# Forward and gradients of a spectral block with an MLP: gradient products laid beside the spectral passes, gelu and slope in one pass, transposes by DMA

## The chip, the cores and the metric

One core of a Trainium2 chip runs the whole program once. The metric is the device time in microseconds (us), as the median of several runs. TensorE (PE) multiplies, VectorE (DVE), ScalarE (ACT) and GpSimd (POOL) work on tiles, and SP, ACT and POOL issue transfers.

## The reference

The kernel computes the block, all in bf16 at its borders, and the gradient of every input but the MLP's own x, for an incoming `grad_out` (S = 2048 tokens, D = 1024, F = 3584):

```python
sa, ca, ga, sb, cb, gb = rows of silu(c) @ w_mod
h  = layernorm(x) * (1 + ca) + sa
x1 = x + ga * irfft2(rfft2(h) * (w_r + 1j * w_i))
h2 = layernorm(x1) * (1 + cb) + sb
out_0 = x1 + gb * (gelu_tanh(layernorm(h2) @ w1 + b1) @ w2 + b2)
# out_1 .. out_9: gradients of x, w_r, w_i, w1, b1, w2, b2, c, w_mod
```

## The kernel before

The spectral filter is done with products: tokens and columns are folded into even and odd parts, a cosine or sine matrix is multiplied from both sides, and the spectrum is handled in eight pairs of row blocks. `spectral` (L357 on) does it for the forward and for the backward: `prep_chunk` and the folds for four chunks of 512 tokens, `s_fwd` (L398, 128 products "pu"), eight times `pair` (L419, products "pcs", then the multiplication by w on DVE; in the backward also the gradients of w), `s_inv` (L484, 128 products "pv"), and for four chunks the products "po" (L511), their copies to `o4` (L513), the unfolding and `consume_chunk`. In the forward, `consume_fwd` (L556 on) forms x1, two layernorms and n3, and stores A, x1, n2 and n3 to DRAM.

The MLP stages follow one after the other, each with its own pools, so that a stage's tiles stand where an earlier one's stood. Six of them have 896 products of 128x512 each:
- z = n3 @ w1 (L623), over four token blocks of 512 and seven groups of four row tiles; n3 is transposed on PE (L103). gelu is done there; z, the sigmoid and gelu's value are stored as d_zb, d_sg and d_hh, and `transpose_sf` (L118 to L122) transposes gelu's value on PE into d_hhs.
- the w2 product (L662), with w2 in SBUF, out_0, and gBo = grad_out * gb.
- gz (L745): gBo times w2 transposed; d_zb and d_sg are loaded again, gelu's slope is computed, `gz` is stored as d_gz and, transposed on PE, as d_gzs.
- the gradients of w2 (L807) and of w1 (L831).
- the gradient of n3 (L859) with `ln_bwd_tile` (L700 to L708).

Then `spectral` runs backward, and `gmod_part` (L761 on; three calls, one of them ahead of L807) forms the gradients of w_mod (L773, an outer product on ACT) and c (L775, a reduction on DVE) from the six rows that stand in d_gmod. The code's order is each engine's order; SP and ACT share the loads, POOL has most stores; w1T and w2T come by DMA transposes on ACT's queue (L786, L687).

Of the kernel before, what the change touches and what calls it, by code (L numbers as in the profile page):

```python
# [10 lines left out]
FP32 = mybir.dt.float32  # L11
# [6 lines left out]
P = 128  # L18
S = 2048
# [16 lines left out]
def kernel(  # L36
# [51 lines left out]
    d_sg = dram.tile([F, S], BF16, name="d_sg")
    d_hhs = dram.tile([S, F], BF16, name="d_hhs")
    d_gzs = dram.tile([S, F], BF16, name="d_gzs")  # L90
    d_gmod = dram.tile([6 * D], FP32, name="d_gmod")
    d_zb_v = d_zb.rearrange("(fc p) s -> p fc s", p=P)
    d_sg_v = d_sg.rearrange("(fc p) s -> p fc s", p=P)
# [3 lines left out]
    def srows(dt, t):  # L97
        return dt[t * P:(t + 1) * P, :]

    def transpose8(src):  # L100
        pt = psum.tile([P, NDC * P], BF16, tag="tr", name="pt")
        for cc in range(NDC):
            nc.tensor.transpose(pt[:, cc * P:(cc + 1) * P], src[:, cc * P:(cc + 1) * P], ident[:])  # L103
        return pt

    def transpose_into(dstT, col0, src):
        pt = transpose8(src)
        nc.vector.tensor_copy(out=dstT[:, 0:NDC, col0:col0 + P],  # L108
                              in_=pt[:, :].rearrange("p (c k) -> p c k", k=P))

    def transpose_sf(wk, src4, d_dst, blk, g):
        stg = wk.tile([P, 4, 4 * P], BF16, tag="stg")
        for ip in range(2):
            pt = psum.tile([P, 2, 4 * P], BF16, tag="pc", name="pts")
            for ii in range(2):
                i = ip * 2 + ii
                for k in range(4):
                    nc.tensor.transpose(pt[:, ii, k * P:(k + 1) * P], src4[:, k, i * P:(i + 1) * P], ident[:])  # L118
            if ip == 0:
                nc.scalar.copy(out=stg[:, 0:2, :], in_=pt[:])  # L120
            else:
                nc.vector.tensor_copy(out=stg[:, 2:4, :], in_=pt[:])  # L122
        nc.sync.dma_start(out=d_dst[blk * BW:(blk + 1) * BW, g * BW:(g + 1) * BW].rearrange("(i p) f -> p i f", p=P),
                          in_=stg[:])

    def store_gmod(wk, accs, r):
        for h in range(2):
            row = wk.tile([1, KH], FP32, tag="gmrow")
            nc.vector.tensor_copy(out=row[:], in_=accs[h][0:1, :])  # L129
            nc.sync.dma_start(out=d_gmod[r * D + h * KH:r * D + (h + 1) * KH].rearrange("(o n) -> o n", o=1), in_=row[:])  # L130

    modx = ExitStack()
    modp = modx.enter_context(tc.tile_pool(name="modp", bufs=1))
    modrows = modp.tile([P, 6, D], BF16, name="modrows")
    modrows_b = const.tile([P, 4, D], BF16, name="modrows_b")
    modcols = const.tile([P, 6, NDC], FP32, name="modcols")
# [3 lines left out]
    with tc.tile_pool(name="modw", bufs=2) as mw:  # L140
        c_bf = mw.tile([P, NDC], BF16, name="c_bf", bufs=1)
        with nc.allow_non_contiguous_dma(reason="tiny c load"):
            nc.sync.dma_start(out=c_bf[:], in_=c.rearrange("o (j p) -> p (o j)", p=P))
        nc.vector.tensor_copy(out=c_col[:], in_=c_bf[:])
        nc.scalar.activation(out=sigc[:], in_=c_col[:], func=ACT.Sigmoid)
        nc.vector.tensor_tensor(out=u_col[:], in0=c_col[:], in1=sigc[:], op=ALU.mult)
        u_b = mw.tile([P, NDC, P], BF16, name="u_b", bufs=1)
        nc.gpsimd.memset(u_b[:], 0.0)
        for jc in range(NDC):
            nc.vector.tensor_scalar(out=u_b[:, jc, :], in0=u_b[:, jc, :], scalar1=u_col[:, jc:jc + 1],  # L150
                                    scalar2=None, op0=ALU.add)
        modraw = mw.tile([P, 6, D], BF16, name="modraw", bufs=1)
        for cb in range(12):
            wblk = mw.tile([P, NDC, KH], BF16, tag="wblk", bufs=3)
            (nc.sync, nc.gpsimd, nc.scalar)[cb % 3].dma_start(
                out=wblk[:], in_=w_mod[:, cb * KH:(cb + 1) * KH].rearrange("(j p) n -> p j n", p=P))
            pm = psum.tile([P, KH], FP32, tag="pa", name="pm")
            for jc in range(NDC):
                nc.tensor.matmul(pm[:], lhsT=u_b[:, jc, :], rhs=wblk[:, jc, :], start=(jc == 0), stop=(jc == NDC - 1))
            nc.scalar.copy(out=modraw[:, cb // 2, (cb % 2) * KH:(cb % 2 + 1) * KH], in_=pm[:])  # L160
        for r in range(6):
            if r in (1, 4):
                nc.vector.tensor_scalar(out=modrows[:, r, :], in0=modraw[:, r, :], scalar1=1.0, scalar2=None,
                                        op0=ALU.add)
            else:
                nc.scalar.copy(out=modrows[:, r, :], in_=modraw[:, r, :])
        pcol = psum.tile([P, 6 * NDC], FP32, tag="pb", name="pcol")
        for r in range(6):
            for dc in range(NDC):
                nc.tensor.matmul(pcol[:, r * NDC + dc:r * NDC + dc + 1], lhsT=modrows[0:1, r, dc * P:(dc + 1) * P],  # L170
                                 rhs=ones_bf[0:1, 0:1], start=True, stop=True)
        nc.vector.tensor_copy(out=modcols[:].rearrange("p r c -> p (r c)"), in_=pcol[:])
    sa_row = modrows[:, 0, :]
    opca_row = modrows[:, 1, :]
    ga_row = modrows[:, 2, :]
    sb_row = modrows[:, 3, :]
    opcb_row = modrows[:, 4, :]
    gb_row = modrows[:, 5, :]
    nc.scalar.copy(out=modrows_b[:, 0, :], in_=modrows[:, 1, :])
    nc.scalar.copy(out=modrows_b[:, 1, :], in_=modrows[:, 4, :])  # L180
    nc.scalar.copy(out=modrows_b[:, 2, :], in_=modrows[:, 5, :])
    nc.scalar.copy(out=modrows_b[:, 3, :], in_=modrows[:, 2, :])
    opca_row_b = modrows_b[:, 0, :]
    opcb_row_b = modrows_b[:, 1, :]
    gb_row_b = modrows_b[:, 2, :]

    d_P = dram.tile([8, P, 4 * PW], BF16, name="d_P")
    d_SF = dram.tile([P, 4, 4, 512], BF16, name="d_SF")
    d_SI = dram.tile([P, 4, 4, 512], BF16, name="d_SI")
    d_E = dram.tile([P, 2, 8, 256], BF16, name="d_E")  # L190
    d_G = dram.tile([P, 2, 8, 256], BF16, name="d_G")
    CE, CO, SE, SO = 0, 1, 2, 3

    with tc.tile_pool(name="dft", bufs=1) as dftp, tc.tile_pool(name="gen", bufs=2) as gen:
        SFg = dftp.tile([P, 4, 4, 512], BF16, name="SFg")
        SIg = dftp.tile([P, 4, 4, 512], BF16, name="SIg")
# [12 lines left out]

        kev = to_f(iota_f([[128, 4], [64, 2], [-1, 64]], 64, 0, 512, "kev"), 512, "kev")  # L210
# [798 lines left out]
```

## Time and profile before

| | us |
|---|---|
| median of three runs (2504.49 to 2512.33) | 2506.34 |
| the profiled execution | 2504.36 |
| its span | 2502.6 |
| PE busy | 1629.9 |
| DVE busy | 1222.0 |
| ACT busy | 622.3 |
| POOL busy | 249.1 |

The span runs from the first to the last instruction of the profiled execution; an engine's busy time leaves out waits. No engine is busy over the whole span, so it has to be read by stages.

### The profile page before, as it was taken

The page shows a single profiled execution, that of the slowest core. Times are in us where ns is not written, and L with a number is a line of the kernel's source. Part 1 is how long each engine was busy: PE and PEld are TensorE (multiplying, and loading weights), DVE is VectorE, ACT ScalarE, POOL GpSimd, SP SyncE. Part 2 cuts the span into 40 slices and gives each one's busy share as a digit, 9 for nine tenths or more (in the row PEclk, how much of TensorE's full clock was granted, in tenths as well). Part 3 has the DMA queues.
Part 4 walks back from the last instruction along what each step waited for, and adds up shares of the span by engine and source line. Part 5 has one row for each costly group of instructions (what it writes and reads, how often), then busy time and mean ns, then how long its engine had stood idle before and what let it go on. Part 6 is the DMA issues. An engine that isn't in the chain of part 4 may idle for free. (4 is left out here: it accounts for less than half of the span.)

```text
span 2502.6 us, 21021 instructions
## 1 busy us (share of the span) xinstructions
PE 1629.9 (65%) x7779; PEld 757.4 (30%) x7928; DVE 1222.0 (49%) x1759; ACT 622.3 (25%) x736; POOL 249.1 (10%) x375
## 2 busy tenths in 40 slices
PE   3108610189983899879995989788889953754200
PEld 1004310044441344334442434333334420322100
DVE  4465776355551111289990000000136557597784
ACT  2304310055551000065540000000012220312332
POOL 1000010011110111111000000111100000030000
PEclk7559855599996999989997989899989985867655
DMA  6643254576669543487779231333165335343355
GB/s 207 171 159 114 89 215 154 193 235 222 224 219 263 155 139 106 138 299 259 254 229 220 83 101 68 130 99 99 43 186 171 105 78 151 115 113 115 121 179 173
DMA packets 295659, 400.06 MB, mean 160 GB/s; under 512 B 98038, under 2 KB 221944, under 8 KB 294276
## 3 DMA queue, kind: packets, MB, share of 16 engines
q1 hardware_dynamic: 153044, 188.32, 24.7%
q0 software_dynamic: 47792, 144.84, 16.5%
q10 hardware_dynamic: 94720, 65.55, 9.9%
q8 instruction: 62, 1.02, 0.2%
q14 instruction: 41, 0.34, 0.0%
HBM read 212.90 MB, written 167.83 MB: 152 GB/s over the span
## 5 line engine op out<-in xcount | busy, mean ns | idle before, releaser
L807 PE MATMUL gw2acc<-gbo_all,hhs 128*128 128x512 bf16 x878 | 210.3, 401 | 42.8 <-ACT ot L813 25.2
L662 PE MATMUL pbo<-w_sb,hhb 128*128 128x512 bf16 x878 | 206.3, 387 | 33.5 <-DMA x1t<-d_x 26.0
L831 PE MATMUL gw1acc<-gzs,n_all 128*128 128x512 bf16 x878 | 202.2, 388 | 29.7 <-DMA gzs<-d_gzs 13.2
L859 PE MATMUL pg<-w1T,gzb 128*128 128x512 bf16 x880 | 200.7, 383 | 19.9 <-DMA gzb<-d_gz 18.9
L623 PE MATMUL pz<-n3T,w_sb 128*128 128x512 bf16 x868 | 204.8, 390 | 5.3 <-DVE n3T L108 3.1
L745 PE MATMUL ph<-gBoT,w2T 128*128 128x512 bf16 x868 | 201.6, 380 | 2.8 <-DVE gBoT L108 1.2
L398 PE MATMUL pu<-smat,fbuf 128*128 128x512 bf16 x251 | 64.9, 416 | 122.5 <-DMA smat<-d_SF 76.6
L807 PEld LDWEIGHTS <-hhs 128*128 128x128 bf16 x896 | 91.2, 102 | 161.6 <-issue 66.3
L814 DVE CAST ot<-gw2acc 128x512 bf16<-128x512 f32 x28 | 18.7, 689 | 237.4 <-PE gw2acc L807 193.5
L831 PEld LDWEIGHTS <-n_all 128*128 128x128 bf16 x896 | 89.3, 100 | 142.7 <-issue 43.7
L662 PEld LDWEIGHTS <-hhb 128*128 128x128 bf16 x896 | 87.6, 100 | 143.4 <-issue 38.1
L859 PEld LDWEIGHTS <-gzb 128*128 128x128 bf16 x896 | 88.2, 99 | 127.4 <-issue 23.0
L838 DVE CAST ot<-gw1acc 128x512 bf16<-128x512 f32 x28 | 19.4, 692 | 217.6 <-PE gw1acc L831 141.5
L623 PEld LDWEIGHTS <-w_sb 128*128 128x128 bf16 x896 | 88.5, 100 | 108.2 <-issue 10.8
L103 PE MATMUL pt<-ident,n3t 128*128 128x128 bf16 x128 | 12.9, 277 | 164.7 <-DMA n3t<-d_n 164.6
L745 PEld LDWEIGHTS <-w2T 128*128 128x128 bf16 x896 | 85.9, 98 | 94.9 <-issue 2.0
L625 ACT ACTIVATE zb<-pz,b_col 128x512 bf16<-128x512 f32 x112 | 75.4, 684 | 111.1 <-PE pz L623 107.1
L484 PE MATMUL pv<-smi,R 128*128 128x512 bf16 x248 | 67.3, 421 | 32.3 <-DVE R L453 18.4
L679 DVE TENSOR_TENSOR gbo<-go,modrows_b 128x1024 bf16<-128x1024 bf16 x16 | 11.1, 693 | 150.9 <-DMA go<-in_grad_out_dram 150.9
L667 ACT CAST bo<-pbo 128x512 bf16<-128x512 f32 x32 | 18.7, 586 | 251.8 <-PE pbo L665 203.4
L813 ACT CAST ot<-gw2acc 128x512 bf16<-128x512 f32 x28 | 15.7, 587 | 237.7 <-PE gw2acc L807 148.1
L398 PEld LDWEIGHTS <-fbuf 128*128 128x128 bf16 x256 | 25.8, 104 | 161.6 <-issue 83.7
(602 smaller groups left out, 2555.7 us busy)
## 6 DMA issues: line engine op xcount, KB each, us to landing
d_zb<-zb POOLq DMA_DIRECT2D x28, 512.0 KB, 5.2
d_sg<-sg POOLq DMA_DIRECT2D x28, 512.0 KB, 3.4
d_hhs<-stg SPq DMA_DIRECT2D x28, 512.0 KB
sg<-d_sg ACTq DMA_DIRECT2D x28, 512.0 KB
zb<-d_zb SPq DMA_DIRECT2D x28, 512.0 KB
d_gz<-gz POOLq DMA_DIRECT2D x28, 512.0 KB, 4.5
d_gzs<-stg SPq DMA_DIRECT2D x28, 512.0 KB
x<-in_A_x_dram SPq DMA_DIRECT2D x32, 256.0 KB
```

The costliest lines, as they stand in the source:

```text
L398: nc.tensor.matmul(pu[:], lhsT=fbuf[:, i, cl, c8 * P:(c8 + 1) * P], rhs=smat[:, cl, i, :], start=(i == 0), stop=(i == 3))
L484: nc.tensor.matmul(pv[:], lhsT=R[:, cl * 4 + m, :, :].rearrange("p x w -> p (x w)")[:, base:base + 255:2], rhs=smi[:, cl, m, :], start=(m ...
L623: nc.tensor.matmul(pz[:], lhsT=w1_sb[:, cch, fc * P:(fc + 1) * P], rhs=n3T[:, cch, :], start=(cch == 0), stop=(cch == NDC - 1))
L625: nc.scalar.activation(out=zb[:, k, :], in_=pz[:], func=ACT.Identity, bias=b1_col[:, fc:fc + 1], scale=1.0)
L662: nc.tensor.matmul(pb_[:], lhsT=hhbs[fc // HF][:, fc % HF, i * P:(i + 1) * P], rhs=w2_sb[:, fc, h * KH:(h + 1) * KH], start=(fc == 0), sto ...
L667: nc.scalar.copy(out=bo[:, h * KH:(h + 1) * KH], in_=pb_[:])
L745: nc.tensor.matmul(ph[:], lhsT=w2T[:, cch, fc * P:(fc + 1) * P], rhs=gBoT[:, cch, :], start=(cch == 0), stop=(cch == NDC - 1))
L807: nc.tensor.matmul(accs[k * 2 + h][:], lhsT=hhs[:, t, k * P:(k + 1) * P], rhs=gbo_all[:, t, h * KH:(h + 1) * KH], start=(t == 0), stop=(t ...
L814: nc.vector.tensor_copy(out=ot[:, KH:D], in_=accs[k * 2 + 1][:])
L831: nc.tensor.matmul(accs[cch][:], lhsT=n3_all[:, t, cch * P:(cch + 1) * P], rhs=gzs[:, t, :], start=(t == 0), stop=(t == NT - 1))
L838: nc.vector.tensor_copy(out=ot[:], in_=accs[cch][:])
L859: nc.tensor.matmul(pg[:], lhsT=gzb[:, fc, i * P:(i + 1) * P], rhs=w1T[:, fc, h * KH:(h + 1) * KH], start=(fc == 0), stop=(fc == NFC - 1))
```

## The change

The file is rewritten, with the same arithmetic in other places:
- All SBUF tiles come from one pool `reg` with tags set by hand, so that a tile of a later stage waits only for the tile whose tag it takes; the tile framework's scheduler orders each engine. PSUM has 2 + 2 + 4 banks under the tags s, d and f.
- gBo and its transposes come first. The product with w2 transposed (`pp`, L573) is placed beside the forward spectral pass and stored as d_ph. POOL generates the matrices' angles.
- `z_block` (L599) computes z, gelu, gelu's slope and gz in one pass; `bo_pass` (L635) runs the w2 product for one block and one half of the columns between z blocks and loads w2 again each time (28 MB in all).
- the gradient of n3 (L720) has the layernorm gradients and the backward fold in its loop. The gradient of w2 (L817) stands after the backward spectral pass in the code, and the scheduler mixes it with that pass's consume. The w_mod gradients (L859, L861) stand ahead of the gradient of w1 (L887).
- n1 and n2 are not stored but computed again; layernorm sums run on ACT (`ln_act`).
- There are no PE transposes: n3, gBo, w1, w2, d_hh and d_gz come transposed by DMA. All transfers but POOL's are on SP.

```diff
-                        nc.scalar.activation(out=zb[:, k, :], in_=pz[:], func=ACT.Identity,
...
-                    nc.scalar.activation(out=sg[:], in_=u_[:], func=ACT.Sigmoid, scale=2.0 * GK)
...
-                    transpose_sf(wk, hh, d_hhs, blk, g)
...
-                        nc.vector.tensor_tensor_reduce(out=gz[:, k, :], in0=ph[:], in1=dd[:, k, :], scale=1.0, scalar=0.0,
...
-                    transpose_sf(wk, gz, d_gzs, blk, g)
...
+    for fg in range(F // 256):
+        w2t = wt[:, fg % 2]
+        nc.sync.dma_start_transpose(out=w2t, in_=B_w2[fg * 256:(fg + 1) * 256, :])
+        for b in range(NB):
...
+            for k in range(2):
...
+                    nc.tensor.matmul(pp[:], lhsT=w2t[:, cch, k * P:(k + 1) * P], rhs=gBoT[b][:, cch, :],
...
+                nc.scalar.copy(out=ph2[:, k, :], in_=pp[:])
...
+            nc.sync.dma_start(out=ph, in_=d_ph_v[:, g * 4:(g + 1) * 4, b * BW:(b + 1) * BW])
...
+            nc.scalar.activation(out=av, in_=zb, func=ACT.Square)
+            nc.vector.tensor_scalar(out=av, in0=av, scalar1=GC, scalar2=1.0, op0=ALU.mult, op1=ALU.add)
+            tt(bv, av, zb, ALU.mult)
+            nc.scalar.activation(out=sg, in_=bv, func=ACT.Sigmoid, scale=2.0 * GK)
+            nc.scalar.activation(out=bv, in_=bv, func=ACT.Sigmoid, scale=-2.0 * GK)
+            nc.vector.tensor_scalar(out=av, in0=av, scalar1=6.0 * GK, scalar2=-4.0 * GK, op0=ALU.mult, op1=ALU.add)
+            tt(hh, sg, zb, ALU.mult)
...
+    z_block(0, 0, 7)
+    bo_pass(0, 0)
+    for b in range(1, NB):
+        z_block(b, 0, 4)
+        bo_pass(b - 1, 1)
+        z_block(b, 4, 7)
+        bo_pass(b, 0)
+    bo_pass(NB - 1, 1)
...
+        nc.sync.dma_start_transpose(out=hhs, in_=d_hh[fg * 256:(fg + 1) * 256, :])
...
+            nc.scalar.activation(out=gw, in_=grep_, func=ACT.Copy, scale=u_rt[:, jc:jc + 1])
...
+        nc.sync.dma_start_transpose(out=gzs, in_=d_gz[fg * 512:(fg + 1) * 512, :])
```

How the orders differ at three places. First PE in the forward consume. Before, the last of the products "po" on the inverse spectrum V are followed by the PE transposes of n3's rows (n3t):

```order
L511 MATMUL po<-gneg,V 128x256
L511 LDWEIGHTS V
L511 MATMUL po<-gneg,V 128x256
L103 LDWEIGHTS n3t
L103 MATMUL pt<-ident,n3t 128x128
```

Now PE has the "pp" products (weights w2 transposed, `wt`) up to the first "po" of the next chunk:

```order
L573 MATMUL pp<-gBoT_340,wt 128x512
L573 LDWEIGHTS wt
L573 MATMUL pp<-gBoT_340,wt 128x512
L464 LDWEIGHTS V_1200
L464 MATMUL po<-gm,V_1200 128x256
L464 LDWEIGHTS V_1200
```

Some 94 "pp" products stand ahead of each of the three later chunks, 68 ahead of the main "pu" run, and 344 in one piece behind the last chunk.

Second, the transposes of w1. Before, ACT's queue issued them between the end of gz and the first copies of the w2 gradient:

```order
L120 COPY stg<-pts 128x1024 x2
L771 DMA wrow<-in_w_mod_dram 128x1024
L786 DMA_TRANSPOSE w1T<-in_B_w_dram 128x1024 x4
L120 COPY stg<-pts 128x1024
L786 DMA_TRANSPOSE w1T<-in_B_w_dram 128x1024 x24
L813 CAST ot<-gw2acc_7965 128x512
```

Now they are on SP, among the last w2 loads of the w2 product (w2sA, w2sB, w2sC):

```order
L694 DMA_TRANSPOSE w1T_5735<-in_B_w_dram 128x1024 x2
L643 DMA w2sA<-in_B_w_dram 128x4x512
L694 DMA_TRANSPOSE w1T_5735<-in_B_w_dram 128x1024
L694 DMA_TRANSPOSE w1T_5740<-in_B_w_dram 128x1024
L643 DMA w2sB<-in_B_w_dram 128x4x512
L694 DMA_TRANSPOSE w1T_5740<-in_B_w_dram 128x1024 x3
```

Third, ACT at the w_mod gradients. Before, they stood at the end of its order, behind the last layernorm gradients (L707), with their own loads:

```order
L773 ACTIVATE gw<-grep__13311,u_rt 128x3072
L707 ACTIVATE tmp<-n_13242,sc 128x1024 x4
L771 DMA wrow<-in_w_mod_dram 128x3072 x2
L771 DMA wrow<-in_w_mod_dram 128x2048
L773 ACTIVATE gw<-grep__13371,u_rt 128x2048 x3
```

Now the 48 outer rows (gww) stand between the first and the second copy of the w1 gradient (gwo):

```order
L837 ACTIVATE sr<-accSA_9560 1x512
L837 ACTIVATE sr<-accSA_9561 1x512
L891 CAST gwo_9802<-gw1acc 128x512
L859 ACTIVATE gww<-gr_9576,u_rt 128x1024 x8
L859 ACTIVATE gww<-gr_9577,u_rt 128x1024 x8
```

Four more such groups of eight follow, and then the other 27 copies in one piece. On DVE, too, few of its 28 copies (L893) stand ahead of its 48 reductions (L861).

More of the change, by code (lines that the diff above doesn't have):

```diff
@@ L88 @@
[L88 to L93, printed above, removed]
-    d_hh_v = d_hh.rearrange("(fc p) s -> p fc s", p=P)
-    d_gz_v = d_gz.rearrange("(fc p) s -> p fc s", p=P)
[L97 to L135, printed above, removed]
@@ L136 @@
-    modcols = const.tile([P, 6, NDC], FP32, name="modcols")
+    rows4 = const.tile([P, 4, D], BF16, name="rows4")
+    opca_row, ga_row, opcb_row, gb_row = (rows4[:, r, :] for r in range(4))
+    stats = const.tile([P, 3, 2, NT], FP32, name="stats")
+    gb1_acc = const.tile([P, NFC, NB], FP32, name="gb1_acc")
     u_col = const.tile([P, NDC], FP32, name="u_col")
@@ L139 @@
     c_col = const.tile([P, NDC], FP32, name="c_col")
[L140 to L184, printed above, removed]
@@ new lines, in tt, with store_gmod, colsum @@
+    def tt(out, a, b, op):
+        nc.vector.tensor_tensor(out=out, in0=a, in1=b, op=op)
+    def store_gmod(accs, r):
+        for h in range(2):
+            row = small.tile([1, KH], FP32, tag="gmrow", bufs=1)
+            nc.vector.tensor_copy(out=row[:], in_=accs[h][0:1, :])
+            nc.sync.dma_start(out=d_gmod[r * D + h * KH:r * D + (h + 1) * KH].rearrange("(o n) -> o n", o=1), in_=row[:])
+    def colsum(accs, src, first, last):
+        for h in range(2):
+            nc.tensor.matmul(accs[h][:], lhsT=ones_bf[:], rhs=src[:, h * KH:(h + 1) * KH], start=first, stop=last)
@@ new lines @@
+    c_bf = small.tile([P, NDC], BF16, tag="c_bf", bufs=1)
+    b1_bf = small.tile([P, NFC], BF16, tag="b1_bf", bufs=1)
+    with nc.allow_non_contiguous_dma(reason="tiny column loads"):
+        nc.sync.dma_start(out=c_bf[:], in_=c.rearrange("o (j p) -> p (o j)", p=P))
+        nc.gpsimd.dma_start(out=b1_bf[:], in_=B_b1.rearrange("(f p) -> p f", p=P))
+    nc.vector.tensor_copy(out=b1_col[:], in_=b1_bf[:])
+    nc.vector.tensor_copy(out=c_col[:], in_=c_bf[:])
+    nc.scalar.activation(out=sigc[:], in_=c_col[:], func=ACT.Sigmoid)
@@ new lines, with mod_block @@
+    MOD_DST = {0: sar[:, 0, 0, :], 1: opca_row, 2: ga_row, 3: sb_row, 4: opcb_row, 5: gb_row}
+    wblkA = reg.tile([P, 4, NDC, KH], BF16, name="wblkA", tag="fr")
+    def mod_block(r, h, wblk):
+        cb = 2 * r + h
+        nc.sync.dma_start(out=wblk, in_=w_mod[:, cb * KH:(cb + 1) * KH].rearrange("(j p) n -> p j n", p=P))
+        pm = ps_f("pm")
+        for jc in range(NDC):
+            nc.tensor.matmul(pm[:], lhsT=u_b[:, jc, :], rhs=wblk[:, jc, :], start=(jc == 0), stop=(jc == NDC - 1))
+        dst = MOD_DST[r][:, h * KH:(h + 1) * KH]
+        nc.scalar.copy(out=dst, in_=pm[:])
+        if r in (1, 4):
+            nc.vector.tensor_scalar(out=dst, in0=dst, scalar1=1.0, scalar2=None, op0=ALU.add)
@@ new lines, in ln_act @@
+    def ln_act(x4, row, i, jk):
+        sv = small.tile([P, 4, 4], FP32, tag="lnsv")
+        for q in range(4):
+            nc.scalar.activation(out=jk[:, q, :], in_=x4[:, q, :], func=ACT.Identity, accum_out=sv[:, q, 0:1])
+        nc.vector.tensor_scalar(out=sv[:, :, 1:2], in0=sv[:, :, 0:1], scalar1=-1.0 / D, scalar2=None, op0=ALU.mult)
+        for q in range(4):
+            nc.scalar.activation(out=jk[:, q, :], in_=x4[:, q, :], func=ACT.Square, bias=sv[:, q, 1:2], accum_out=sv[:, q, 2:3])
+        ln_fin(sv[:, :, 2:3], sv[:, :, 1:2], sv[:, :, 3:4], 1.0 / D, row, i)
@@ new lines, in ln_fin, with ln_dve @@
+    def ln_fin(var, nmean, std, scale, row, i):
+        nc.scalar.activation(out=std, in_=var, func=ACT.Sqrt, bias=eps_c[:], scale=scale)
+        rs = stats[:, row, 0, 4 * i:4 * i + 4].rearrange("p (q o) -> p q o", o=1)
+        nc.vector.reciprocal(out=rs, in_=std)
+        tt(stats[:, row, 1, 4 * i:4 * i + 4].rearrange("p (q o) -> p q o", o=1), nmean, rs, ALU.mult)
+    def ln_dve(x4, row, i):
+        st = small.tile([P, 4, 2, nc.vector.BN_STATS_DIM], FP32, tag="lnst")
+        mv = small.tile([P, 4, 4], FP32, tag="lnmv")
@@ new lines, in ln_dve, with norm_act, s_fwd @@
+        ln_fin(mv[:, :, 1:2], mv[:, :, 2:3], mv[:, :, 3:4], 1.0, row, i)
+    def norm_act(out4, in4, row, i):
+        for q in range(4):
+            t = 4 * i + q
+            nc.scalar.activation(out=out4[:, q, :], in_=in4[:, q, :], func=ACT.Identity,
+                                 scale=stats[:, row, 0, t:t + 1], bias=stats[:, row, 1, t:t + 1])
+    def s_fwd(cl, fb, sm, evac):
+        Ut = reg.tile([P, 8, 512], BF16, name=f"U{cl}", tag=f"uv{cl}")
+        for c8 in range(8):
+            pu = ps_s("pu")
+            for i in range(4):
+                nc.tensor.matmul(pu[:], lhsT=fb[:, i, cl, c8 * P:(c8 + 1) * P], rhs=sm[:, i, :],
+                                 start=(i == 0), stop=(i == 3))
+            evac(Ut[:, c8, :], pu[:])
+        return Ut
@@ new lines @@
+    for fg in range(F // 256):
+        hhs = hhs2[fg % 2]
+        nc.sync.dma_start_transpose(out=hhs, in_=d_hh[fg * 256:(fg + 1) * 256, :])
+        for k in range(2):
+            fc = 2 * fg + k
+            ob = gwo[:, fc % 2]
+            for h in range(2):
+                acc = ps_f("gw2acc")
+                for t in range(NT):
+                    nc.tensor.matmul(acc[:], lhsT=hhs[:, t, k * P:(k + 1) * P], rhs=gBs[t // 4][:, t % 4, h * KH:(h + 1) * KH],
+                                     start=(t == 0), stop=(t == NT - 1))
+                nc.scalar.copy(out=ob[:, h * KH:(h + 1) * KH], in_=acc[:])
+            nc.gpsimd.dma_start(out=out_6[fc * P:(fc + 1) * P, :], in_=ob)
@@ new lines @@
+    accGA = [ps_f("accGA0"), ps_f("accGA1")]
+    for b in range(NB):
+        gxa = reg.tile([P, 4, D], BF16, name="gxa", tag=f"uv{2 * (b % 2)}")
+        ata = reg.tile([P, 4, D], BF16, name="ata", tag=f"uv{2 * (b % 2) + 1}")
+        nc.sync.dma_start(out=gxa[:], in_=chunk_rows(d_gx1, b))
+        nc.sync.dma_start(out=ata[:], in_=chunk_rows(d_A, b))
+        tt(gxa[:], gxa[:], ata[:], ALU.mult)
+        for q in range(4):
+            colsum(accGA, gxa[:, q, :], b == 0 and q == 0, b == 3 and q == 3)
@@ new lines @@
+    for fg in range(F // 512):
+        gzs = gzs2[:, fg % 2]
+        nc.sync.dma_start_transpose(out=gzs, in_=d_gz[fg * 512:(fg + 1) * 512, :])
+        for cch in range(NDC):
+            acc = ps_f("gw1acc")
+            for t in range(NT):
+                nc.tensor.matmul(acc[:], lhsT=n3ns[t // 4][:, t % 4, cch * P:(cch + 1) * P], rhs=gzs[:, t, :],
+                                 start=(t == 0), stop=(t == NT - 1))
+            ob = gwo1[:, (fg * NDC + cch) % 4]
+            if cch % 2 == 0:
+                nc.scalar.copy(out=ob, in_=acc[:])
+            else:
+                nc.vector.tensor_copy(out=ob, in_=acc[:])
+            nc.gpsimd.dma_start(out=out_4[cch * P:(cch + 1) * P, fg * 512:(fg + 1) * 512], in_=ob)
```

1306 lines of the change are left out of this document (593 added, 713 removed).

## The prediction

> **What bounds the kernel now.** I read the page's head, then a table of busy time by stage that I cut at the changes of line in TensorE's (PE's) timeline, then the groups, then single waits.
>
> ```profile
> span 2502.6 us, 21021 instructions
> PE 1629.9 (65%) x7779; PEld 757.4 (30%) x7928; DVE 1222.0 (49%) x1759; ACT 622.3 (25%) x736; POOL 249.1 (10%) x375
> ```
>
> No engine is full over the span: PE idles 873 us. In the table the columns are the stretch, its length, busy time of PE, weight loads, DVE, ACT, POOL, then PE's granted clock, DMA share and GB/s.
>
> ```profile
> 0.00:194.00 194.00, 40.75 (x161) 14.57 (x165) 101.60 (x186) 37.08 (x43) 14.91 (x23) 0.61 0.59 174
> 194.00:297.00 103.00, 90.31 (x417) 47.17 (x423) 66.00 (x94) 45.73 (x82) 4.29 (x8) 0.94 0.34 111
> 297.00:487.00 190.00, 12.81 (x73) 8.87 (x72) 127.36 (x192) 13.09 (x29) 14.61 (x17) 0.54 0.51 185
> 487.00:773.00 286.00, 244.47 (x1441) 126.44 (x1469) 148.53 (x155) 153.09 (x169) 42.17 (x56) 0.91 0.68 223
> 773.00:1046.00 273.00, 228.30 (x976) 95.68 (x995) 42.17 (x66) 19.38 (x33) 27.78 (x42) 0.92 0.50 139
> 1046.00:1317.00 271.00, 235.75 (x1444) 120.30 (x1471) 248.21 (x399) 142.30 (x91) 30.33 (x46) 0.95 0.80 263
> 1317.00:1583.00 266.00, 210.57 (x884) 91.28 (x899) 19.97 (x31) 16.73 (x29) 23.87 (x38) 0.87 0.44 118
> 1583.00:1821.00 238.00, 202.21 (x878) 89.26 (x896) 19.37 (x28) 16.41 (x28) 34.74 (x61) 0.94 0.29 96
> 1821.00:2134.00 313.00, 233.53 (x984) 99.85 (x1004) 187.46 (x287) 62.77 (x97) 13.96 (x19) 0.85 0.45 132
> 2134.00:2260.00 126.00, 90.66 (x347) 42.46 (x353) 93.14 (x125) 36.68 (x65) 31.57 (x50) 0.81 0.45 118
> 2260.00:2400.00 140.00, 39.01 (x182) 21.16 (x185) 109.59 (x134) 52.44 (x61) 5.05 (x5) 0.62 0.39 136
> 2400.00:2502.00 102.00, 1.55 (x4) 0.30 (x2) 58.64 (x66) 26.57 (x14) 5.84 (x11) 0.50 0.50 169
> ```
>
> Row by row: head; forward transforms; forward consume; z; w2 product; gz; gw2; gw1; gn3 with the backward fold; backward transforms; backward consume; grad-w_mod tail. Six product stages are PE's; head, both consumes and tail leave it 153, 177, 101 and 100 us idle.
>
> ```profile
> 486.91 1.33 PE L103 MATMUL pt<-ident,n3t 128*128 128x128 bf16 x11 [144.79 <-DMA n3t<-d_n]
> 580.65 6.42 PE L623 MATMUL pz<-n3T,w_sb 128*128 128x512 bf16 x28
> ```
>
> The first row is the largest single wait: 144.79 us. The second gives the steady product: 6.42/28 = 0.229 us, so each 896-matmul stage costs 205 us.
>
> **The change, in stages.** *Removed:* the gz stage as a stage (271 us), since its product goes under the forward spectral pass, and these PE transposes (39.9 us busy; 12.9 and 11.0 us of L103's go too):
>
> ```profile
> L118 PE MATMUL pts<-ident,gz 128*128 128x128 bf16 x448 | 39.9, 224 | 23.0 <-DVE gb_acc L747 21.9
> ```
>
> *Head, 150 us (130 to 180; was 194).* The forward matrix no longer goes out to d_SF and back:
>
> ```profile
> L398 PE MATMUL pu<-smat,fbuf 128*128 128x512 bf16 x251 | 64.9, 416 | 122.5 <-DMA smat<-d_SF 76.6 <-DVE fbuf L383 29.9 <-DVE fbuf L273 14.8
> ```
>
> Of that 76.6 us I take 44 back, because four gBo transposes and 68 pp products now stand ahead of the main pu run.
>
> *Transforms, 112 us (103 to 130; was 103).* A pair is two products of 2052 columns and six of about half that on DVE, 2 x 1.23 + 6 x 0.69 = 6.6 us:
>
> ```profile
> L445 DVE TENSOR_TENSOR qb<-Pt,ws 128x2052 bf16<-128x2052 bf16 x16 | 19.7, 1229 | 0.0
> L447 DVE TENSOR_TENSOR Q<-qa,qb 128x1026 bf16<-128x1026 bf16 x16 | 11.1, 694 | 0.0
> ```
>
> So 128 pu at 0.229 are 29, eight pairs 53, 128 pv 29. PE's pp work fits in the pairs' gaps; without that cover it would be late by what stands there, some 110 products or 25 us, which is the upper end.
>
> *Forward consume, 218 us (190 to 260; was 190).* Here a serial chain of ACT and DVE, a chunk at a time, is the pace, since o4 and x4 have one buffer each. On ACT, now the engine of the mean, square and normalising passes, these rows price it:
>
> ```profile
> L513 ACT CAST o<-po 128x512 bf16<-128x512 f32 x64 | 33.6, 619 | 69.9 <-DMA out_dram<-o 33.4 <-DMA d_A<-o 29.7 <-DMA out_dram<-gw 4.2
> L707 ACT ACTIVATE tmp<-n2t,sc 128x1024 bf16<-128x1024 bf16 x16 | 19.8, 1240 | 10.1 <-DVE sc L704 10.1
> L861 ACT ACTIVATION_READ_ACCUMULATOR gn<-pg 128x1 f32 x32 | 6.2, 194 | 0.0
> L285 DVE TENSOR_TENSOR tmp<-o 128x2048 bf16<-128x2048 bf16 x8 | 9.7, 1208 | 6.7 <-ACT o L513 6.7
> L392 ACT CAST U<-pu 128x512 bf16<-128x512 f32 x48 | 27.8, 587 | 84.7 <-PE pu L398 83.2 <-remote 1.4
> ```
>
> The chain of a chunk: unfold 8 x 1.21, two products of 4096 columns 4 x 1.21, mean and square passes 8 x (1.24 + 0.194), normalising 4 x 1.24, the next o4's copies 8 x 0.619, and some 12 copies of pp banks at 0.587 between them in ACT's order: 9.7 + 4.8 + 11.5 + 5 + 5 + 7 = 43, with waits about 45. Three periods and the last po make 139; the 344 pp products that stand densely behind it take 344 x 0.229 = 79. So z starts near 480, as now (487), but the 205 us of w2-transposed products lie behind it.
>
> *z with the w2 product, 485 us (440 to 540; was 286 + 273).* PE needs 1792 x 0.229 = 410 plus 15 of small sums. Of a group of four z tiles, DVE has five tensor products and two scalar passes of 2048 columns and four reductions: 5 x 1.21 + 2 x 1.08 + 4 x 0.77 = 11.3 us, against 14.7 us of PE; ACT 4 x 0.684 + 3 x 2.0 = 8.7.
>
> ```profile
> L625 ACT ACTIVATE zb<-pz,b_col 128x512 bf16<-128x512 f32 x112 | 75.4, 684 | 111.1 <-PE pz L623 107.1 <-remote 3.0 <-DVE q__2142 L629 0.9
> L735 ACT ACTIVATE om<-sg,ones_f 128x2048 bf16<-128x2048 bf16 x28 | 56.0, 2001 | 72.4 <-DMA sg<-d_sg 52.4 <-DMA n_all<-d_n 19.9
> L540 DVE TENSOR_SCALAR n<-x,mv 128x1024 bf16<-128x1024 bf16 x32 | 15.3, 541 | 0.0
> L747 DVE CUSTOM_DVE_ANT_0 gz<-ph,m__7412 128x512 bf16<-128x512 f32 x4 | 2.7, 689 | 0.0
> L747 DVE DVE_READ_ACCUMULATOR2_ANT gb_acc<- 128x1 f32 x112 | 9.6, 85 | 0.0
> ```
>
> But the order gives runs of three to seven z groups and then a whole w2 pass of 112 x 0.229 = 25.6 us. Each group's chain (two ACT passes, three DVE ones, the sigmoids, five more on DVE) is some 20 us and there are two slots, so the z runs go at DVE's pace: 7 x (11.3 - 7.3) = 28 us for the first seven groups, which nothing covers, and some 4 for each of three later blocks. The w1T transposes stand among the last w2 loads in SP's order, and what they delay is PE: I take 20. So 410 + 15 + 28 + 12 + 20 = 485. All covered but the first run it is near 440; with every run at DVE's pace, 540.
>
> *gn3, 272 us (255 to 313; was 313).* 896 products and 64 sums are 220. Behind the last chunk's products DVE still has eight norm gradients of 1.30 + 0.41 + 1.28 us, four reductions of 1.30, three products of 2 x 1.21 and a fold of 8 x 1.21: 24 + 5 + 7 + 10 = 46, and 6 of ACT.
>
> ```profile
> L700 DVE CUSTOM_DVE_ANT_0 junk<-gn,n2t 128x1024 bf16<-128x1024 bf16 x16 | 19.6, 1223 | 0.5
> L708 DVE SCALAR_TENSOR_TENSOR gh<-gn,stats,tmp 128x1024 bf16<-128x1024 bf16 x16 | 20.6, 1284 | 21.6 <-ACT tmp L707 21.6
> ```
>
> Earlier chunks' DVE work lies beside the next chunk's 55 us of PE.
>
> *Backward transforms, 140 us (126 to 165; was 126)*: as forward, with two more of each size for grad w, 10.4 us a pair: 29 + 83 + 29. No pp or gw2 product stands between them in PE's order.
>
> *Backward consume with gw2, 245 us (226 to 285; was 140 and 266).* PE 205 + 14 + 7 = 226; the serial chain of a chunk (o4, unfold 9.7, four norm gradients of about 5.5, loads, store) is near 50 with one o4 buffer: 4 x 50 = 200, so PE is the bound, with waits.
>
> *gw1 with the tail, 290 us (239 to 320; was 238 and 102).* ACT's order has one gw1 copy, then all 48 outer rows, then the other 27 copies; PE has four banks, so it holds after five or six accumulators (20 us).
>
> ```profile
> L773 ACT ACTIVATE gw<-grep__7905,u_rt 128x1024 bf16<-128x1024 f32 x8 | 9.1, 1144 | 0.1
> L775 DVE CUSTOM_DVE_ANT_0 wrow<-wrow,gbf 128x1024 bf16<-128x1024 bf16 x8 | 9.8, 1222 | 0.4 <-DMA wrow<-in_w_mod_dram 0.4
> out_dram<-gw POOLq DMA_DIRECT2D x8, 256.0 KB, 6.0
> ```
>
> 48 x 1.144 = 55 on ACT, 48 x 1.30 = 62 on DVE; with four buffers and a landing of 6.0 us, at most 48 x 1.95 = 94. I take 60, and 25 for the last modulation sums ahead: 205 + 60 + 25.
>
> Sum: 150 + 112 + 218 + 485 + 272 + 140 + 245 + 290 = 1912. The profiled run took 2504.36, 1.8 over its span, and the median 2506.34 is 2.0 above that: **1916**, say 1920.
>
> **Transposes by DMA.** These are the unknown resource: 57 MB (d_hh and d_gz 14.7 each, w1, w2 7.3 each, the rest small) against 17 before.
>
> ```profile
> 772.72 49.04 ACTq L687 DMA_TRANSPOSE w2T<-in_B_w_dram  x5
> 1319.87 53.83 ACTq L786 DMA_TRANSPOSE w1T<-in_B_w_dram  x24
> 1340.00:1350.00 10.00, 9.95 (x47) 4.51 (x46) 0.00 (x0) 0.00 (x0) 0.00 (x0) 1.00 1.07 236
> 1350.00:1360.00 10.00, 9.95 (x47) 4.54 (x47) 0.00 (x0) 0.00 (x0) 0.00 (x0) 1.00 1.17 169
> 1360.00:1370.00 10.00, 4.18 (x19) 1.83 (x19) 1.29 (x2) 0.00 (x0) 0.00 (x0) 0.81 1.11 135
> ```
>
> 5 x 0.917 MB in 49.04 is 94 GB/s, 24 x 0.262 MB in 53.83 is 117; in three stretches of that run with a full DMA share, 236, 169 and 135 GB/s move. gw2 needs 1.05 MB per 64 products (14.7 us), gw1 2.1 MB per 128: 71 GB/s, below the slowest row. So I hide them, with 20 us exposed for w1T.
>
> The Trainium skill's page "Advanced Engine Details and Errata" (X-Bar Transpose (TRN2)) says that transposes are as fast as ordinary transfers, 350 to 400 GB/s. The trace disagrees, with 94 and 117 for the two runs of them; what a higher rate would bring here is the fourth rival.
>
> **Rivals.** (1) *In-order queues stall more than I charge.* Consume 55 us a chunk (+40 forward, +30 backward), z's chains not covered by the w2 passes (+55), the 48 rows at the landing's pace (+35): 1916 + 160 = 2076. For it: every engine's order is fixed and o4 has one buffer; against it: ACT and DVE have room in z. (2) *Fuller overlap.* PE's 1630 less 64 of transposes is 1566; 120 in the head and 80 at borders give 1765. (3) *Slower than before.* One queue, SP's, carries all transposes and most loads; were a transpose to move at 30 GB/s there, gw2 and gw1 (29.4 MB) would take 980 instead of 535, w1T 243 instead of 20, the head's 4.2 MB 100 more: 1916 + 445 + 223 + 100 = 2680. It decides below about 35 GB/s, a third of the slowest row. (4) *Transposes at a plain load's rate.* At the 236 GB/s of the best stretch the 20 us for w1T go, and four gBo transposes of 1.05 MB take 4.4 us instead of 9 each, half of that on the head's path: 1916 - 20 - 9 = 1887; against it, both runs of them in the trace.
>
> **How the numbers follow.** Forecast 0.52; stalls 0.24; fuller overlap 0.14; faster transposes 0.05; slower 0.04; within 0.3% (what a measurement of this kernel can tell from no change) 0.01. The term bounds sum to 1709 and 2193; all will not err alike, so the range runs from the fuller overlap to a little beyond the stalls, 1760 to 2110, and leaves out the slower case and the far ends of those two.
>
> **What would show it.** Main pu run near 150 and z near 480; no PE gap over 25 us in the forward consume; z to gn3 near 485; ACT with 48 gw rows in one piece and PE idle about 60 us at gw1's start. A gw2 or gw1 that waits for its transposes throughout, or PE idle in the consumes as long as before, makes the forecast wrong.

## The result, and the profile after

The changed kernel takes 2037.8 us (median of four runs, 2022.19 to 2041.68) beside 2505.4 before in the same runs: a ratio of 0.8114, 95% interval 0.8075 to 0.8153. The forecast was 1920, range 1760 to 2110. The profiled execution took 2022.19, the quickest of the four; its span is 2020.1. Its stages, cut where I cut those of before (main pu run, end of the inverse transform, main z run, first gn3 product, and so on; columns as there):

```profile
0.00:226.00 226.00, 65.06 (x206) 23.95 (x207) 73.42 (x98) 85.80 (x124) 43.56 (x64) 0.65 0.67 162
226.00:338.00 112.00, 104.89 (x475) 52.30 (x474) 50.23 (x69) 60.32 (x106) 8.13 (x14) 0.97 0.58 166
338.00:576.00 238.00, 192.23 (x876) 89.63 (x874) 97.59 (x120) 139.68 (x232) 38.84 (x54) 0.90 0.63 163
576.00:1043.00 467.00, 413.49 (x1837) 178.77 (x1835) 302.34 (x446) 246.75 (x228) 63.25 (x85) 0.97 0.73 202
1043.00:1326.00 283.00, 224.45 (x972) 97.47 (x971) 173.31 (x246) 79.60 (x114) 9.44 (x9) 0.87 0.51 147
1326.00:1461.00 135.00, 94.87 (x384) 45.14 (x384) 78.09 (x102) 54.23 (x95) 31.38 (x50) 0.81 0.51 133
1461.00:1746.00 285.00, 230.47 (x1051) 106.74 (x1050) 125.18 (x160) 86.44 (x121) 26.31 (x43) 0.90 0.62 151
1746.00:2020.00 274.00, 206.56 (x930) 92.08 (x928) 89.03 (x141) 71.89 (x79) 56.61 (x105) 0.88 0.60 178
```

| stage | forecast | measured | difference |
|---|---|---|---|
| head | 150 | 226 | +76 |
| transforms | 112 | 112 | 0 |
| forward consume with the pp products | 218 | 238 | +20 |
| z with the w2 product | 485 | 467 | -18 |
| gn3 with the fold | 272 | 283 | +11 |
| backward transforms | 140 | 135 | -5 |
| backward consume with gw2 | 245 | 285 | +40 |
| gw1 with the tail | 290 | 274 | -16 |
| sum | 1912 | 2020 | +108 |

The saving came from where it was forecast: the gz stage is gone, and PE works 192 of 238 us in the forward consume where it worked 13 of 190. Four stages are 147 us over the forecast and three are 39 under it, so part of the error cancels. Most of it is in two stages, the head and the backward consume. Two rows of waits in the head (us in total, times, longest), the row of SP's timeline for the loads of grad_out (start, time in which SP was at them) and two stretches of 5 us show what it waited for:

```profile
DVE go L158 <- DMA go<-in_grad_out_dram: 50.9, 4, 21.4
ACT n L311 <- DMA x<-in_A_x_dram: 36.2, 8, 8.4
63.01 28.91 SPq L132 DMA_DIRECT2D go<-in_grad_out_dram  x8
75.00:80.00 5.00, 0.00 (x0) 0.00 (x0) 0.00 (x0) 3.02 (x4) 0.96 (x2) 0.50 0.13 52
80.00:85.00 5.00, 0.00 (x0) 0.10 (x1) 0.00 (x0) 0.00 (x0) 0.00 (x0) 0.50 0.13 50
```

SP is held, and yet the DMA engines are 13% busy, which is two of sixteen, at 50 GB/s. The loads of L132 are those of token rows; two of a chunk's four run in descending order. Their access pattern is two groups of 64 rows (`[[64 * D, 2], [-D, 64], [1, w]]`). A 256 KB load of that kind is 5.2 us at 50 GB/s, and eight chunks (four of grad_out, four of x), 16 such loads, stand in the head: by this estimate 84 us of a queue that carries everything else too. **Theory A:** these transfers run on two engines and hold SP's queue. **Theory B:** the four gBo transposes and SP's order as such hold it.

### The profile page after: what moved, and what is told of

The parts are those of the page before. It is cut to its first block, busy times and chain, and to the rows that moved or that the text cites. A ratio compares the mean times of both kernels' runs of the same rounds, so it can differ in the third digit from the quotient of the medians.

```text
span 2020.1 us, 18395 instructions
## 1 busy us (share of the span) xinstructions
PE 1532.0 (76%) x6722; PEld 686.1 (34%) x6722; DVE 989.2 (49%) x1381; ACT 824.7 (41%) x1095; POOL 277.5 (14%) x423
## 5 line engine op out<-in xcount | busy, mean ns | idle before, releaser
L887 PE MATMUL gw1acc<-gzs,n3n 128*128 128x512 bf16 x896 | 199.3, 386 | 59.9 <-ACT gwo L891 43.8
L573 PE MATMUL pp<-gBoT,wt 128*128 128x512 bf16 x896 | 209.9, 392 | 31.4 <-ACT phr L575 15.9
L720 PE MATMUL pg<-w1T,gzr 128*128 128x512 bf16 x896 | 201.9, 386 | 4.9 <-DMA gzr<-d_gz 4.8
L887 PEld LDWEIGHTS <-n3n 128*128 128x128 bf16 x896 | 89.0, 99 | 169.8 <-issue 67.3
L158 DVE TENSOR_TENSOR ct<-ct 128x2048 bf16<-128x2048 bf16 (+1 forms) x76 | 103.4, 1388 | 85.5 <-ACT ct L466 62.6
L573 PEld LDWEIGHTS <-wt 128*128 128x128 bf16 x896 | 90.9, 102 | 142.6 <-issue 29.9
L720 PEld LDWEIGHTS <-gzr 128*128 128x128 bf16 x896 | 89.1, 100 | 115.7 <-issue 8.6
L158 DVE TENSOR_TENSOR gt<-gt,gt 128x2048 bf16<-128x2048 bf16 x84 | 101.9, 1222 | 19.0 <-ACT gt L619 18.1
L612 PE MATMUL pz<-n3Tb,w 128*128 128x512 bf16 x448 | 101.8, 383 | 6.0 <-ACT gt L614 6.0
L817 PE MATMUL gw2acc<-gB,hhsA 128*128 128x512 bf16 x448 | 102.9, 390 | 3.7 <-DMA hhsA<-d_hh 3.7
L817 PE MATMUL gw2acc<-gB,otl 128*128 128x512 bf16 x448 | 102.0, 386 | 3.4 <-ACT gwo L819 3.4
L612 PE MATMUL pz<-n3Ta,w 128*128 128x512 bf16 x448 | 99.9, 379 | 5.5 <-ACT gt L614 5.5
L893 DVE CAST gwo<-gw1acc 128x512 bf16<-128x512 f32 x28 | 19.3, 690 | 148.1 <-PE gw1acc L887 148.1
```

The costliest lines, as they stand in the source:

```text
L158: nc.vector.tensor_tensor(out=out, in0=a, in1=b, op=op)
L573: nc.tensor.matmul(pp[:], lhsT=w2t[:, cch, k * P:(k + 1) * P], rhs=gBoT[b][:, cch, :], start=(cch == 0), stop=(cch == NDC - 1))
L612: nc.tensor.matmul(pz[:], lhsT=w1s[cch][:, fc * P:(fc + 1) * P], rhs=n3T[:, cch, :], start=(cch == 0), stop=(cch == NDC - 1))
L720: nc.tensor.matmul(pgs[i][:], lhsT=gzt[g][:, k, i * P:(i + 1) * P], rhs=w1Ts[g][:, k, h * KH:(h + 1) * KH], start=(g == 0 and k == 0), sto ...
L817: nc.tensor.matmul(acc[:], lhsT=hhs[:, t, k * P:(k + 1) * P], rhs=gBs[t // 4][:, t % 4, h * KH:(h + 1) * KH], start=(t == 0), stop=(t == N ...
L887: nc.tensor.matmul(acc[:], lhsT=n3ns[t // 4][:, t % 4, cch * P:(cch + 1) * P], rhs=gzs[:, t, :], start=(t == 0), stop=(t == NT - 1))
```

## The experiments

### Rows ascending: A against B

```diff
-            out.append((bass.AP(tensor=th, offset=off + r0 * D, ap=[[64 * D, 2], [-D, 64], [1, w]]), t4[:, q, :]))
+            out.append((bass.AP(tensor=th, offset=off + (r0 - 63) * D, ap=[[D, 128], [1, w]]), t4[:, q, :]))
```

> The changed kernel with the loads and stores of token rows in ascending instead of descending order (the reversal of the rows is left out; bytes and counts stay). In the profile, stretches of some 5 us with a DMA share of 0.13 at 50 GB/s go with these transfers. Theory A (a descending transfer runs on two of the 16 DMA engines and all that is behind it on SP's queue waits, which made the head 226 us instead of 150 and the backward consume 285 instead of 245): main pu run at 165 to 190, backward consume 250 to 265, total 70 to 110 us less, about 1950 median. Theory B (the head is held by the four gBo transposes and SP's order): main pu run within 10 us of 226, total within 15 us.

Measured: 1893.2 us (ratio to before 0.7562, 0.7539 to 0.7585), 145 under the changed kernel and more than I expected. Its stages, from the head to the main z run, then gn3, then the backward consume:

```profile
0.00:156.00 156.00, 63.86 (x205) 23.06 (x206) 77.03 (x98) 84.96 (x124) 47.63 (x64) 0.70 0.94 234
156.00:270.00 114.00, 105.28 (x475) 52.42 (x474) 50.22 (x69) 60.60 (x106) 8.37 (x14) 0.96 0.57 163
270.00:500.00 230.00, 189.71 (x874) 89.11 (x873) 97.60 (x120) 140.47 (x231) 38.90 (x54) 0.90 0.59 169
...
964.00:1219.00 255.00, 218.40 (x973) 95.63 (x974) 173.53 (x246) 79.76 (x115) 8.92 (x9) 0.92 0.54 167
...
1355.00:1616.00 261.00, 225.12 (x1051) 105.46 (x1051) 124.99 (x160) 85.97 (x121) 23.97 (x43) 0.94 0.65 164
```

The head falls by 70 us to 156 and its DMA share rises from 0.67 to 0.94; gn3 falls by 28, the backward consume by 24, the forward consume by 8. Together these are 130 us and not 145, for the profiled execution of the changed kernel is 16 us under its median. B as it was put, with the main pu run within 10 us of 226, falls. The four gBo transposes are still there, and SP is at them for 42 of these 156 us; no run takes them out, so what they cost the head stays open:

```profile
45.08 42.11 SPq L511 DMA_TRANSPOSE gBoT<-d_gBo  x4
```

### Two groups of ascending rows: why they are slow

```diff
-            out.append((bass.AP(tensor=th, offset=off + r0 * D, ap=[[64 * D, 2], [-D, 64], [1, w]]), t4[:, q, :]))
+            out.append((bass.AP(tensor=th, offset=off + (r0 - 63) * D, ap=[[D, 2], [2 * D, 64], [1, w]]), t4[:, q, :]))
```

> The changed kernel with the token rows in ascending order, but read as two groups of 64 (first the even, then the odd rows of the same 128; the rows' order is left out). It tells apart why the descending transfers are slow. Theory A1 (the slowest dimension of the access pattern has the size 2, so that two of the 16 DMA engines carry it): as slow as the changed kernel, 2020 to 2045. Theory A2 (descending addresses are slow by themselves): as fast as the ascending one, 1885 to 1905.

Measured: 2032.0 us (0.8107, 0.8087 to 0.8127): 139 of the 145 us are back though no address descends, and so is the stretch of the profile:

```profile
80.00:85.00 5.00, 0.00 (x0) 0.10 (x1) 0.00 (x0) 0.00 (x0) 0.00 (x0) 0.50 0.13 50
```

It is the two groups, the size 2 of the slowest dimension, and not the direction. (The rows of a group are also two rows apart here, which no run varies alone; the share of two engines in sixteen speaks for the size.) The Trainium skill's page "DMA: Bandwidth & Descriptors" (Why a DMA increments its semaphore by 16 and not by 1) says that a transfer is given the largest number of engines, up to 16, that divides the slowest dimension of both its sides: by that rule two here. The trace agrees, with 0.13 of sixteen engines.

### The control: the kernel before with ascending rows

The edit is the same at its loads and stores.

> The kernel before with the token rows ascending (the reversal is left out), the control. If these transfers cost the change more than they cost the kernel before, because the change put them ahead of everything on one queue, this gains less than the 145 us of the changed kernel: I expect 2420 to 2480, by its head (two of the four x loads there) and its backward consume. If it gains as much or more, 2360 or under, the transfers were no part of the error of the forecast's stages, only of both kernels.

Measured: 2413.7 us (0.9629, 0.9607 to 0.9651), 93 under before, a little under the span that I expected. So the kernel before paid for these transfers too, and the change raised the bill by about half, from 93 to 145. Most of that rise is the head: before, the ascending rows shorten it from 194 to 169 us, by 25, and after the change by 70. This is the head of before with ascending rows, and what DVE waits there for x's rows, first with the two groups, then without:

```profile
0.00:169.00 169.00, 40.30 (x161) 14.43 (x165) 101.82 (x186) 36.99 (x43) 14.91 (x23) 0.66 0.63 200
```

```profile
DVE st L531 <- DMA x<-in_A_x_dram: 25.5, 5, 8.0
DVE st L531 <- DMA x<-in_A_x_dram: 7.8, 4, 6.4
```

Without these transfers on either side the ratio is 1893.2 / 2413.7 = 0.784 instead of 0.811.

### The same loads on POOL's queue

```diff
-        for dr, sb in tok_aps(src, t4, i, c0, c1):
-            eng.dma_start(out=sb, in_=dr)
+        for n_, (dr, sb) in enumerate(tok_aps(src, t4, i, c0, c1)):
+            (eng if n_ < 2 else nc.gpsimd).dma_start(out=sb, in_=dr)
```

> The changed kernel with only the descending row loads (two of the four loads of a token chunk) issued by POOL instead of SP; the same result. Theory A: SP's queue is no longer blocked, the head shortens by 30 to 60 us unless POOL's own order (matrix angles, stores) delays these loads; total 1960 to 2010. Theory B: within 15 us. If POOL's queue is what then waits, slower than 2038.

Measured: 2004.8 us (0.8003, 0.7974 to 0.8032). The total is within theory A's span, but not by the way that it gave: the head loses only 14 us (main pu run at 212) where 30 to 60 were expected, and the backward consume stays at 288. There ACT waits 28 us for x's rows, where it waited 30 in the changed kernel, so from POOL's queue they come no sooner. In the head SP is now at the four gBo transposes for twice the time, first in the changed kernel, then in this one; why, I have not settled:

```profile
105.33 33.89 SPq L511 DMA_TRANSPOSE gBoT<-d_gBo  x4
65.12 69.18 SPq L511 DMA_TRANSPOSE gBoT<-d_gBo  x4
```

### Transposes replaced by plain loads

```diff
-        nc.sync.dma_start_transpose(out=hhs, in_=d_hh[fg * 256:(fg + 1) * 256, :])
+        nc.sync.dma_start(out=hhs.rearrange("p t f -> p (t f)").rearrange("p (h s) -> p h s", h=2), in_=d_hh[fg * 256:(fg + 1) * 256, :].rearrange("(h p) s -> p h s", p=P))
```

and likewise for d_gz and w1.

> The changed kernel with the transposes of d_hh, d_gz and w1 by DMA replaced by plain loads of the same bytes (the transposition is left out). Forecast (transposes are hidden but for some 20 us at w1): the w1 part, 24 us of PE waiting in the last w2 pass, goes to under 10; the w2 and w1 gradients keep their times within 5; total 10 to 25 us less. Rival (transposes hold the queue in many places): over 40 us less. Rival (they cost nothing): within 6.

Measured: 2035.3 us (0.8119, 0.8090 to 0.8148), no difference from the changed kernel: the forecast of 10 to 25 us less fell, and the rival by which these transposes cost nothing held. The w2 and w1 gradients keep their times (282 and 273 us, 285 and 274 before the edit). In the last w2 pass PE waits 19 us for w2, where it waited 23; these are its two longest waits, first in this kernel, then in the changed one:

```profile
1007.91 6.49 PE L647 MATMUL pbo<-w2sA,hhA 128*128 128x512 bf16 x16 [8.85 <-DMA w2sA<-in_B_w_dram]
1020.08 5.54 PE L647 MATMUL pbo<-w2sB,hhA 128*128 128x512 bf16 x16 [5.67 <-DMA w2sB<-in_B_w_dram]
```

```profile
1013.47 5.71 PE L647 MATMUL pbo<-w2sA,hhA 128*128 128x512 bf16 x16 [13.22 <-DMA w2sA<-in_B_w_dram]
1022.09 3.61 PE L647 MATMUL pbo<-w2sB,hhA 128*128 128x512 bf16 x16 [2.90 <-DMA w2sB<-in_B_w_dram]
```

So the 20 us charged there are real, but they are not the transposing. They are probably the 7.3 MB of w1 in the same queue among w2's loads, for in the changed kernel's earlier passes, without w1, PE waits for w2 at most 2.9 us at a time; no run takes w1 out of the queue.

### The rows of the w_mod gradient handed out one by one

```diff
-    for ri, r in enumerate((5, 3, 4, 1, 2, 0)):
...
+            if todo:
+                gmod_row()
```

The second piece stands at the end of gw1's loop body. In the changed kernel PE's and ACT's timelines show the hold:

```profile
1791.67 5.73 PE L887 MATMUL gw1acc<-gzs,n3n 128*128 128x512 bf16 x16 [15.63 <-DVE gwo L893]
1841.17 19.09 PE L887 MATMUL gw1acc<-gzs,n3n 128*128 128x512 bf16 x74 [43.76 <-ACT gwo L891]
```

```profile
1839.50 1.15 ACT L859 ACTIVATE gww<-gr,u_rt 128x1024 bf16<-128x1024 f32 x1 [0.56 <-DMA out_dram<-gww]
1840.55 1.05 ACT L891 CAST gwo<-gw1acc 128x512 bf16<-128x512 f32 x2
```

> The changed kernel with the 48 rows of the w_mod gradient handed out one after each accumulator of the w1 gradient instead of all ahead of it; ACT's order then has some six rows between two copies. Theory (PE holds 59 us at the start of the w1 gradient because ACT's and DVE's fixed orders have the rows ahead of the copies): the hold falls to 20 to 35 us, total 25 to 45 us less, about 2000 median. Rival (the rows' stores and loads, DMA share 0.9 there, are the bound, so the wait moves to the w1 gradient's own transposes or to its end): within 15 us.

Measured: 2017.7 us (0.8056, 0.8021 to 0.8091), 20 less where 25 to 45 were expected; the rival's bound was 15. The hold of 59 us (two waits, 15.63 and 43.76) becomes five waits of 2 to 12, 34 us together, of which these are the two longest:

```profile
1809.44 8.75 PE L881 MATMUL gw1acc<-gzs,n3n 128*128 128x512 bf16 x32 [11.76 <-ACT gwo L885]
1864.93 13.46 PE L881 MATMUL gw1acc<-gzs,n3n 128*128 128x512 bf16 x48 [9.89 <-ACT gwo L885]
```

So both causes seem to act. Order made the long hold; in what is left, ACT's rows wait 40 us for their own stores to land, where they waited 22 in the changed kernel, and the copies stand behind them.

### Rows turned on PE, and half of the w_mod rows beside gw2

In the first the rows come ascending, in one group of 128, and are turned by a product with an exchange matrix:

```diff
+                nc.tensor.matmul(pr[:], lhsT=exch[:], rhs=src4[:, q, h * KH:(h + 1) * KH], start=True, stop=True)
+                cp(dst4[:, q, h * KH:(h + 1) * KH], pr[:])
```

> The changed kernel, same result, with token rows loaded ascending and turned on TensorE by a product with an exchange matrix (four products of 512 columns and four copies per chunk), at the head, at the n3 gradient and in the backward consume, with out_1 turned the same way. By theory A nearly all of the 145 us of the ascending run come back less the copies (16 chunks with some 2.5 us on DVE or ACT): 1900 to 1940. If the turning's copies stand in the way of the chains, 1960 to 2000.

> e6_turn with 24 of the 48 rows of the w_mod gradient beside the end of the w2 gradient and the other 24 handed out beside the w1 gradient. If the hold at the w1 gradient is order (ACT's and DVE's rows ahead of the copies), it falls from 59 us to under 15 and the total is 35 to 55 us under e6_turn; if it is the rows' traffic beside the transposes, it moves to the w2 gradient's end: within 20 us of e6_turn.

Measured: 1956.8 us (0.7804, 0.7790 to 0.7819), between the two spans, and 1924.2 us (0.7666, 0.7632 to 0.7700), 33 less, just short of the 35 to 55. The turning gives 58 us of the head back (main pu run at 168) and 20 us of gn3; the backward consume stays at 287, and DVE waits 24 us in it for the turning products. With half of the rows beside gw2, gw1 takes 243 us instead of 279 and its longest hold is one of 15.73 us.

### The backward consume's loads ahead

```diff
+        n1 = reg.tile([P, 4, D], BF16, name="n1b", tag=("sma", "smb")[i % 2])[:]
+        load_tok(nc.sync, n1, A_x, i)
+        nc.sync.dma_start(out=gx, in_=chunk_rows(d_gx1, i))
```

> The changed kernel with x for the backward consume loaded and normalised ahead, into the two tiles that the spectral matrices leave free (before, one buffer took x and then gx1 in turn), same result. Theory (in the changed kernel's backward consume, 285 us, a chunk's period of 57 to 61 us holds the wait for x's descending loads and for gx1 in one buffer): period 45 to 50, stage 250 to 265, total 20 to 35 us less. Rival (the period is DVE's and ACT's work and the store of out_1 from the one o4): within 10 us.

> e7_both with the same loads ahead, same result. Theory: the stage falls from 289 to 250 to 265 us and the total is 1890 to 1905. Rival: within 10 us of 1924.

Measured: 2054.4 us alone (0.8194, 0.8160 to 0.8229), slower by 17; 1916.1 us (0.7634, 0.7601 to 0.7666) with turned rows, within the rival's bound. The stages are 308 and 298 us, where they were 285 and 289. SP's timeline says why the first became slower: the x loads, now ahead, hold the queue for 34 us, and the transpose that gw2 needs stands behind them:

```profile
1472.51 34.28 SPq L132 DMA_DIRECT2D n1b<-in_A_x_dram  x7
1508.56 0.37 SPq L774 DMA_DIRECT2D ct<-d_gx  x1
1508.97 0.55 SPq L132 DMA_DIRECT2D n1b<-in_A_x_dram  x1
1509.62 22.52 SPq L811 DMA_TRANSPOSE hhsA<-d_hh  x1
```

PE waits 20 us there for transposed rows of d_hh, where it waited 4, and ACT waits even longer for x, 41 us instead of 30. So the first run did not take the wait for x away and does not test the theory. The second does: no engine waits for gx1 any more (18 us of DVE in e7_both) and 5 us of waits for x are left, yet the stage is no shorter. There the theory fell; PE now waits 16 us for ACT's copies of gw2's results, 17 for its copies of po and 8 for d_hh.

## Why the prediction was right, and where it was not

- *The direction, and most of the size*, came from the right place: PE's idle time by stage, the 205 us of a product stage, and the order that puts them together. The saving was 468 us, 585 were forecast.
- *How much the two-group transfers explain.* Without them the changed kernel takes 1893, 27 under the forecast, but that nearness is luck: the forecast was built on times of before, which have 93 us of them. Like with like, the saving without them is 2413.7 - 1893.2 = 520 us, still 65 short of 585. So the 52 us by which the change raised their cost are less than half of the 118 by which the forecast missed the median; the rest are other terms.
- *Head, 150 us, measured 226: the step that failed.* "Of that 76.6 us I take 44 back" fails twice. It counted what left the queue and not what came onto it: four chunks of grad_out, with eight two-group loads, now stand among x's, all of them ahead of x's last two chunks, and the two-group loads cost the head 70 us where they cost 25. That is 45 of the 76. The other 31 are the saving itself: with ascending rows on both sides the head falls from 169 to 156, by 13 and not by 44. In this head the DMA engines are 94% busy and SP is at the gBo transposes for 42 us; which of them holds it, no run separates. The warning was in the trace of before, in the 25.5 us that DVE waits for x's rows, which the forecast passed over.
- *Backward consume, 245 us, measured 285.* 24 us are the same transfers. In the ascending run the stage is 261, and PE works 225 of them, as forecast; the term that was too small is the waits, 36 us where 19 were taken. 20 of these are on ACT's copies of po, and 12 on DVE ahead of the column sums (accCA). What would shorten that chain is open: in the one run that took the waits for x and gx1 away, the stage did not shrink.
- *Forward consume, 218, measured 238.* Two mis-sized counts. The period is 39 us, not 45 (one o4 copy after L311 starts at 369.78, 408.92 and 447.83), so the three chunks and the last po take 124 us instead of 139. And 448 pp products stand behind the last chunk, not 344, for 96 precede the first z products and 8 stand among them: with some 10 us of ACT's waits for pp's stores they take 114 us instead of 79.
- *z, 485, measured 467; gn3, 272, measured 283; transforms, 112 and 140, measured 112 and 135.* All are within their bounds. gn3 has 28 us of the two-group loads in it and would be 255.
- *gw1, 290, measured 274:* the hold was 59 us where 60 were taken; the 25 us for the sums ahead were some 10.
- *Transposes.* Hidden as forecast, and the 71 GB/s that gw2 and gw1 need were met: gw2 waits 4 us for them and gw1 not at all. The rivals that rest on them fall. The slow one needed less than about 35 GB/s and the fast one 236; the four gBo transposes, 1.05 MB each, hold SP for 33.89 us, 8.5 each where 9 were taken, which is 124 GB/s, and for w1 plain loads change nothing.
- *The rival of stalling orders*, 2076, is near the median by its time and only in part by its terms. Its 40 for the forward consume came as 20, its 30 for the backward one as 40, of which 24 are the two-group loads; its 55 in z and 35 at the rows did not come, and the 76 of the head are not among its terms.
- *The signs.* The 48 rows in one piece, PE's hold of about 60 us, z to gn3 (467) and no gap of PE over 25 us in the forward consume came as named; main pu run and main z run, at 226 and 576 instead of 150 and 480, did not.

The best kernel, 1916 us, is 6% under the changed one; its interval overlaps that of the kernel with 1924.

## What to carry to other kernels

Look at DMA share and GB/s together in every stretch where an engine waits for a load. Here a low share with a held queue was a transfer on two engines, and its price was paid by all that was queued behind it. Give a transfer a long slowest dimension (128 rows instead of 2 groups were worth 145 us here), and where the order of the data forbids it, load in the easy order and turn on another engine (81 us here). When everything moves to one queue, count what is added to it, not only what leaves. And when a fault is found behind a missed forecast, take it out of the kernel before as well: here that showed that it explained less than half of the miss.

## What was not expected of the hardware

Two descending groups of 64 rows and two ascending ones move at the same 50 GB/s, with 0.13 of the DMA engines busy; the same rows in one group of 128 leave the head at a share of 0.94 and 234 GB/s. Issued by POOL the two-group loads keep ACT waiting as long in the backward consume (28 us beside 30). Transposing d_hh, d_gz and w1, 37 MB, by DMA costs this kernel no more than plain loads of the same bytes (2037.8 beside 2035.3 us).
